# Retention, then a two-layer network, on one core: the last sums reordered and stored in halves, and the last tokens' input copied by two engines

## The chip, the cores and the metric

The kernel runs on one core of a Trainium2 chip. A core has TensorE (matrix products into PSUM), VectorE, ScalarE, GpSimd and SyncE, each with an instruction queue of its own that is worked off in order; engines wait for one another by semaphores. DMAs are issued here from the queues of SyncE and ScalarE (and GpSimd, early on). The metric is the time of one execution on the device, in microseconds (us).

## The reference

```python
def _attn_ref(q, k, v):                       # 8 x 8 x 576 x 64, float32
    scores = (1.0 / np.sqrt(D_)) * np.matmul(q, k.transpose(0, 1, 3, 2))
    gamma = 1.0 - 2.0 ** (-5.0 - np.arange(H))
    Dmat = np.where(rel >= 0, gamma[:, None, None] ** rel[None, :, :], 0.0)   # rel = pos_i - pos_j
    return np.matmul(scores * Dmat[None], v)

def _moe_ref(x, w_in, w_out, alpha):          # x: 4608 x 512, the heads side by side
    h = x @ w_in                              # 4608 x 2048
    s = np.sin(alpha * h)
    g = h + s * s / (alpha + 1e-09)
    return g @ w_out                          # 4608 x 512
```

So each token goes through a causal retention (decay per head), and then through two matrix products with a snake activation between them.

## The kernel before

**Blocks.** The 4608 tokens are worked in nine blocks of 512. Blocks 0 to 7 are the first 512 tokens of each of the eight sequences; block 8, the "ends", gathers the last 64 tokens of all eight. For each block the retention makes the transposed input of the network: `xT` (for block 8 `xS`, four slabs of 128 x 512 in float16). The network's first product runs in 16 units of 128 hidden features (`project`, L554, matmuls on L562): four matmuls of 128x512 sum up one PSUM bank `hps`. ScalarE takes the sine of it (`sine`, L570), ScalarE or VectorE squares that (`square`, L579/L581), and VectorE makes `gT = ss * inva + hps` (`product`, L586), in float16.

**The second product** of blocks 3 to 8 is made from seven products of quarter size instead of eight (`part_product`, L659, matmuls on L671; `FACTORS` names the two factors of each). `row_sum` (L644, VectorE on L652) makes the sums of `gT` that four of the seven take as left factor, and `after_product` (L700) puts the results together: product 1 becomes `low` (ScalarE, L703), product 6 gives `mid = acc + low` (L705), product 7 gives a new `low` (L707), and products 2, 3, 4 and 5 each complete one quarter of the block's output in a tile `osb` (L720), which `store` (L677) sends to the output in two DMAs, one for each half of the partitions (issued on L684 for block 8, on L688 for the others). With `more=True`, used once, product 5 is also added to `mid` (L716), for product 3's quarter needs it: `osb(3) = acc(3) + mid`.

**Order.** The whole kernel lies in a manual schedule: each engine's instructions stand in the order in which the program names them. A loop over blocks n = 3 to 8 names, for each pair of units, the first product of block n and one quarter-size product of block n - 1. `unit_start` (L1351) issues a unit's matmuls and sine and whatever `at_unit` has put there; `unit_end` (L1357) issues the square, the `product`, and then what `behind` has put there. In block 7 the retention of the ends is made (class `Ends`, L469): `Ends(0)` covers four sequences, `Ends(2)` the other four, each with a PSUM tile of its own. At unit 13 their matmuls are issued (L510 and L528), and L1348 puts the four copies from PSUM into `xS` (`keep`, L535, through `copy`, L118; L120 on ScalarE, L122 on VectorE) behind units 13 and 14: the two of `Ends(0)` behind unit 13, the two of `Ends(2)` behind unit 14, all on ScalarE. Block 8's first `project` reads all of `xS`. In block 7, unit 14 ends only after unit 15 has started and the quarter-size product 4 of block 6 has been handled (L1398 to L1404).

**The end** (L1406 to L1427) makes the seven products of block 8 with no first product left beside them, in the order 2, 4, 1, 6, 7, 5, 3. Stores there are issued from two queues, `both` = SyncE's for partitions 0 to 63 and ScalarE's for 64 to 127. Product 3 is made in two column halves (js = 0, 1) in two PSUM banks; VectorE sums each half into `osb(3)` as it is finished, and one `store` behind both sends the 128 x 512 tile: two DMAs of 64 partitions x 2 x 256 float32, 128 KB each.

Of the kernel before, what the change touches and what calls it, by code (L numbers as in the profile page):

```python
# [12 lines left out]
ADD = mybir.AluOpType.add  # L13
# [23 lines left out]
def kernel(  # L37
# [18 lines left out]
    nc = tc.nc  # L56
# [49 lines left out]
    V, A_, G_ = nc.vector, nc.scalar, nc.gpsimd  # L106
# [8 lines left out]
    def halves(n):  # L115
        return slice(64 * n, 64 * n + 64)
# [542 lines left out]
    def part_product(n, i, tag, js=(0, 1), first=None):  # L659
        left, right = FACTORS[i]  # L660
        if tag is not None:
            parts[n, i] = bank(tag)
        else:
            parts[n, i] = parts[n, first]
        acc = parts[n, i]
        for j in js:
            for p in range(2):
                lhs = piece(left, p) if isinstance(left, str) else quarter(n, *left, p)
                rhs = piece(right, p) if isinstance(right, str) else w_quarter(*right, p)
                for x in range(4):  # L670
                    matmul(  # L671
                        acc[:, 256 * j : 256 * j + 256], lhs[:, x, 128 * j : 128 * j + 128], rhs[:, x],
                        start=(tag is not None and j == js[0] and p == 0 and x == 0),
                        stop=(p == 1 and x == 3), skip_group_check=True,
                    )

    def store(n, t, e, osb, js=(0, 1), issue=(nc.sync, nc.sync)):  # L677
        cols = slice(256 * e, 256 * e + 256)
        for r in range(2):
            if n == 8:  # L680
                b0 = 4 * t + 2 * js[0]
                dst = out.rearrange("(b s) d -> b s d", s=S)[b0 : b0 + 2 * len(js), 512:576, cols]
                dst = dst.rearrange("(j r) s d -> r s j d", r=2)
                issue[r].dma_start(dst[r], osb[halves(r), js[0] : js[-1] + 1])  # L684
            else:
                r0 = 576 * n + 256 * t + 128 * js[0]
                dst = out[r0 : r0 + 128 * len(js), cols].rearrange("(j i r) d -> r i j d", r=2, i=64)
                issue[r].dma_start(dst[r], osb[halves(r), js[0] : js[-1] + 1])  # L688

    kept = {}  # L690
# [4 lines left out]
    def kept_tile(name):  # L695
        tag = {"low": "qT1", "mid": "u2"}[name]
        kept[name] = work.tile([P, 512], F32, tag=tag, bufs=1, name=name)
        return kept[name]

    def after_product(n, i, js=(0, 1), issue=(nc.sync, nc.sync), apart=False, more=False):  # L700
        acc = parts[n, i]
        if i == 1:
            nc.scalar.copy(kept_tile("low"), acc)  # L703
        elif i == 6:
            nc.vector.tensor_tensor(kept_tile("mid"), acc, kept["low"], ADD)  # L705
        elif i == 7:
            nc.vector.tensor_tensor(kept["low"], acc, kept["mid" if apart else "low"], ADD)  # L707
        else:
            t, e = {2: (0, 0), 3: (0, 1), 4: (1, 0), 5: (1, 1)}[i]
            cols = slice(256 * js[0], 256 * js[-1] + 256)  # L710
            if (n, i) not in kept:
                kept[n, i] = work.tile([P, 2, 256], F32, tag="osb", bufs=4, name="osb")
            osb = kept[n, i].rearrange("p j d -> p (j d)")
            source = kept["mid" if i == 3 else "low"]
            if more:
                nc.vector.tensor_tensor(kept["mid"], acc, kept["mid"], ADD)  # L716
            if i == 2 and not apart:
                nc.scalar.copy(osb[:, cols], acc[:, cols])
            else:
                nc.vector.tensor_tensor(osb[:, cols], acc[:, cols], source[:, cols], ADD)  # L720
            if issue:
                store(n, t, e, kept[n, i], js, issue)

    at = [Attention(b) for b in range(B)]
    zero = work.tile([P, 512], F16, tag="zero", bufs=1, name="zero")
# [57 lines left out]
    with tc.manual_schedule():  # L783
# [485 lines left out]
        for n in range(3, NBLK):  # L1269
# [4 lines left out]
            def at_unit(u, *fs):  # L1274
                todo.setdefault(u, []).extend(fs)

            def behind(u, *fs):
                after.setdefault(u, []).extend(fs)
# [59 lines left out]
            if n == 7:  # L1338
                for i in range(PAD):
                    at_unit(3 + i, fill_up)  # L1340
                E = (Ends(0), Ends(2))
                at_unit(7, lambda: E[0].scores(next(m)), lambda: E[1].scores(next(m)))
                at_unit(7, E[0].masked)
                behind(7, E[1].masked)
                at_unit(13, lambda: E[0].values(False, next(m)), lambda: E[1].values(False, next(m)))
                at_unit(13, lambda: E[0].values(True), lambda: E[1].values(True))
                at_unit(13, E[0].add_states, E[1].add_states)
                for i in range(4):  # L1348
                    behind(13 + i // 2, lambda i=i: E[i // 2].keep(i % 2, A_))

            def unit_start(i, u, tag):  # L1351
                project(n, u, tag)
# [38 lines left out]
            for i in range(8):  # L1391
                for u in (2 * i, 2 * i + 1):
                    unit_start(u, units[u], aside.get(u) or next(h))
                    if u % 2 and slots[i] is not None:
                        k_ = slots[i]
                        part_product(n - 1, k_, None if k_ in (2, 7, 3) else "op", first={2: 1, 7: 6, 3: 5}.get(k_))
                        after_product(n - 1, k_)
                    if n < 8 and u == 14:  # L1398
                        square(n, u, A_)
                        continue  # L1400
                    if n < 8 and u == 15:
                        product(n, 14)
                        for f in after.get(14, []):
                            f()  # L1404
                    unit_end(u, units[u], None if A and u == 13 else V if u in ON_V else A_)
        n = NBLK - 1  # L1406
        both = (nc.sync, nc.scalar)
# [3 lines left out]
        row_sum(n, "S2", 1, V)  # L1411
        part_product(n, 1, "op")
        after_product(n, 1)
        part_product(n, 6, next(h))
        row_sum(n, "S1", 1, V)
        after_product(n, 2, apart=True, issue=both)
        row_sum(n, "S4", 1, V)
        after_product(n, 6)
# [4 lines left out]
        after_product(n, 5, more=True, issue=both)  # L1423
        for j, tag in enumerate(("m0", "op")):
            part_product(n, 3, tag, (j,))
            after_product(n, 3, (j,), None)
        store(n, 0, 1, kept[n, 3], issue=both)  # L1427


# [28 lines left out]
```

## Time and profile before

| what | value |
|---|---|
| time, three runs | 296.99, 298.12 (the median), 298.87 us |
| the profiled execution | 297.58 us, of which the span from first to last instruction is 295.9 us |
| mean granted TensorE clock | 0.996 |
| busy: PE / VectorE / ScalarE / GpSimd | 283.5 / 225.0 / 204.9 / 135.9 us |
| busy from 252 to 291 us (39 us: block 8) | PE 38.43, VectorE 32.70, ScalarE 18.82 us |
| from 291 us to the end (4.9 us) | PE 0, VectorE 0.28 us |

How the lines of a profile are read: times are us from the start of the span, durations in us or ns where marked. In a timeline, a row gives start, duration, engine, line, operation, output tile <- input tiles, shapes, and how many instructions are merged in the row (x8); brackets at its end give the idle time of the engine just before the row and who ended it. PE is TensorE's matmul row, PEld its weight loads (which run ahead of the matmuls), DVE is VectorE, ACT ScalarE, POOL GpSimd, SPq and ACTq the DMA-issuing queues of SyncE and ScalarE. A group line of the page gives busy time and mean duration after the bar. Matmuls overlap one another and their ends are modelled, so the distance between two starts says more than a duration.

### The profile page before, as it was taken

How to read it: one execution, taken by the hardware profiler on the slowest of the kernel's cores; microseconds unless marked ns; L12 is line 12 of the kernel's file. 1: busy time of each engine (PE TensorE's matmuls, PEld its weight loads, DVE VectorE, ACT ScalarE, POOL GpSimd, SP SyncE). 2: the span in 40 equal slices, each digit the busy share in tenths (PEclk: the TensorE clock that was granted, in tenths of full speed). 3: DMA queues.
4: the chain of work that ended last, by engine and by line, in shares of the span. 5: the costliest groups of instructions: out<-in, count | busy, mean ns of one | idle time of the engine just before them, and what ended most of it. 6: DMA issues, size and time to landing. Idle time of an engine off the chain costs nothing.

```text
span 295.9 us, 8497 instructions
## 1 busy us (share of the span) xinstructions
PE 283.5 (96%) x3480; PEld 183.5 (62%) x3480; DVE 225.0 (76%) x334; ACT 204.9 (69%) x343; POOL 135.9 (46%) x151
## 2 busy tenths in 40 slices
PE   6789999999999999999999999999999999999993
PEld 4566545555544644455777767767767776676782
DVE  2596978788348889697977697769777986977883
ACT  2579935997594887786767976887688657865500
POOL 5693678565688685560497049704950000000000
PEclk9999999999999999999999999999999999999998
DMA  7999999998798778999979777988753103111213
GB/s 216 347 234 210 248 296 321 243 259 241 177 226 176 175 164 174 253 161 194 146 178 218 147 168 189 218 146 198 179 133 79 40 13 78 35 38 35 71 38 107
DMA packets 123400, 50.09 MB, mean 169 GB/s; under 512 B 80353, under 2 KB 121313, under 8 KB 123361
## 3 DMA queue, kind: packets, MB, share of 16 engines
q1 hardware_dynamic: 119424, 44.78, 65.1%
q0 software_dynamic: 2688, 4.19, 7.8%
q10 hardware_dynamic: 1248, 0.58, 0.7%
q8 instruction: 27, 0.44, 0.6%
q14 instruction: 13, 0.10, 0.1%
HBM read 36.75 MB, written 9.44 MB: 156 GB/s over the span
## 4 chain that ended last, share of the span: by engine, by line
PE 80%; DMA 10%; POOL 3%; ACT 3%; SPq 1%; issue 1%; DVE 0%; POOLq 0%; ACTq 0%
PE hps L562 39%; PE hps L671 24%; PE ops L605 9%; DMA raw<-in_v_dram 3%; DMA w_in<-in_moe_w_in_dram 3%; PE o L427 2%; DMA raw<-in_k_dram 2%; PE sc L385 2%; DMA qT<-q 2%; PE kv L321 1%; POOL q L207 1%; ACT s L570 1%; POOL k L207 1%; PE o L449 1%; SPq L158 1%
## 5 line engine op out<-in xcount | busy, mean ns | idle before, releaser
L586 DVE SCALAR_TENSOR_TENSOR gT<-ss,inva,hps 128x512 f16<-128x512 f16 x144 | 105.7, 744 | 31.1 <-ACT ss L579 27.5
L570 ACT ACTIVATE s<-hps,alpha_t 128x512 f16<-128x512 f32 x144 | 96.8, 680 | 46.0 <-PE hps L562 45.7
L562 PE MATMUL hps<-xT,w_in 128*128 128x512 f16 (+1 forms) x532 | 121.0, 372 | 0.5 <-DMA w_in<-in_moe_w_in_dram 0.5
L562 PEld LDWEIGHTS <-w_in 128*128 128x128 f16 x596 | 66.6, 114 | 50.3 <-DMA w_in<-in_moe_w_in_dram 0.6
L579 ACT ACTIVATE ss<-s 128x512 f16<-128x512 f16 x107 | 67.3, 630 | 2.8
L605 PE MATMUL ops<-w_out,gT 128*128 128x512 f16 x192 | 46.8, 380 | 0.0
L671 PEld LDWEIGHTS <-gT 128*128 128x128 f16 x384 | 37.5, 98 | 8.3
L207 POOL TENSOR_TENSOR k<-raw,cn 128x1024 f16<-128x1024 f32 (+1 forms) x17 | 29.6, 1746 | 8.5 <-DMA raw<-in_k_dram 8.5
L671 PEld LDWEIGHTS <-S 128*128 128x128 f16 x288 | 27.7, 98 | 5.3
L605 PEld LDWEIGHTS <-gT 128*128 128x128 f16 x192 | 17.9, 98 | 20.4
L359 POOL TENSOR_TENSOR s<-kvs,cn 128x256 f16<-128x256 f32 x17 | 10.4, 612 | 38.9 <-DVE S L652 36.0
L207 POOL TENSOR_TENSOR q<-raw,cn 128x1024 f16<-128x1024 f32 x13 | 24.9, 1919 | 7.3 <-DMA raw<-in_q_dram 4.3
L671 PE MATMUL hps<-T,gT 128*128 128x256 f16 x192 | 22.9, 273 | 0.0
L671 PE MATMUL hps<-w_out,gT 128*128 128x256 f16 x192 | 22.9, 273 | 0.0
L671 PE MATMUL hps<-w_out,S 128*128 128x256 f16 x192 | 22.8, 273 | 0.0
L397 DVE TENSOR_TENSOR ret<-sc,mask 128x1024 f16<-128x1024 f32 x16 | 19.2, 1220 | 1.9 <-PE sc L385 1.9
L367 POOL TENSOR_TENSOR kvs<-s,kvs 128x256 f32<-128x256 f32 x21 | 16.7, 797 | 3.6 <-DVE kvs L122 1.1
L720 DVE TENSOR_TENSOR osb<-hps,low 128x512 f32<-128x512 f32 x13 | 9.0, 691 | 10.6 <-PE hps L671 10.6
L581 DVE TENSOR_TENSOR ss<-s 128x512 f16<-128x512 f16 x29 | 13.4, 465 | 3.4 <-ACT s L570 3.4
L366 POOL TENSOR_TENSOR s<-kvs,cn 128x256 f32<-128x256 f32 x21 | 12.8, 612 | 6.6 <-ACT kvs L120 6.4
L652 DVE TENSOR_TENSOR S<-gT,S 128x1024 f16<-128x1024 f16 x24 | 15.5, 684 | 0.0
L562 PE MATMUL hps<-xS,w_in 128*128 128x512 f16 x64 | 15.1, 379 | 0.4 <-ACT xS L120 0.4
(82 smaller groups left out, 270.7 us busy)
## 6 DMA issues: line engine op xcount, KB each, us to landing
out_dram<-osb SPq DMA_DIRECT2D x68, 128.0 KB, 2.6
raw<-in_q_dram SPq DMA_DIRECT2D x16, 512.0 KB, 6.3
raw<-in_k_dram SPq DMA_DIRECT2D x8, 512.0 KB, 5.9
raw<-in_v_dram SPq DMA_DIRECT2D x8, 512.0 KB, 6.4
raw<-in_v_dram SPq DMA_DIRECT2D x32, 128.0 KB, 3.1
raw<-in_k_dram SPq DMA_DIRECT2D x32, 128.0 KB, 3.1
w_in<-in_moe_w_in_dram POOLq DMA_DIRECT2D x4, 512.0 KB, 11.6
w_out<-in_moe_w_out_dram POOLq DMA_DIRECT2D x4, 512.0 KB, 12.9
```

What stands on the lines that cost most here:

```text
L207: eng.tensor_tensor(dst[:, a0:a1].rearrange("p a r t d -> p t (a r) d"), t_.rearrange("p (t a) x -> p t a x", t=2)[:, :, a0:a1].rearrange( ...
L366: nc.gpsimd.tensor_tensor(s32, self.kvs[:, c - 1], g1.unsqueeze(2).to_broadcast([P, 4, D]), MULT)
L367: nc.gpsimd.tensor_tensor(self.kvs[:, c], s32, self.kvs[:, c], ADD)
L397: nc.vector.tensor_tensor(ret.rearrange("p t (z x) -> p (t z) x", z=2)[:, :, 0:n], sc.rearrange("p t (z x) -> p (t z) x", z=2)[:, :, 0:n], ...
L562: matmul(hps_of[n, fc][0][:, cols], w_in16[fc // 4][:, a, fc % 4 :: 4], xs[n][:, a, cols], start=(a == 0 and part != 1), stop=(a == KT - 1 ...
L570: nc.scalar.activation(s_t, hps, mybir.ActivationFunctionType.Sin, bias=0.0, scale=alpha_t[:, fc : fc + 1],)
L579: nc.scalar.activation(ss_t, s_t, mybir.ActivationFunctionType.Square)
L581: eng.tensor_tensor(ss_t, s_t, s_t, MULT)
L586: nc.vector.scalar_tensor_tensor(gT[n][:, fc, :], ss_t, inva[:, fc : fc + 1], hps, MULT, ADD)
L605: matmul(ops[n, c, cols.start][:, cols], gT[n][:, fk, c * P : (c + 1) * P], w_out16[:, fk, cols], start=(fk == 0), stop=(fk == FC - 1), sk ...
L652: return eng.tensor_tensor(out_, x, y, op)
L671: matmul(acc[:, 256 * j : 256 * j + 256], lhs[:, x, 128 * j : 128 * j + 128], rhs[:, x], start=(tag is not None and j == js[0] and p == 0 ...
```

## The change

Three things are edited.

1. In `after_product`, VectorE's addition to `mid` (only with `more`, product 5 of block 8) comes behind product 5's own sum and its store, not ahead of them.
2. Product 3 of block 8 stores each column half as soon as its sum is made: two times two DMAs of 64 partitions x 256 float32 (64 KB each), in place of two DMAs of 128 KB behind both halves.
3. The two `xS` copies of `Ends(2)` go from ScalarE to VectorE, and from behind unit 14 of block 7 to behind unit 13, where those of `Ends(0)` stand and stay. On VectorE they come behind the first half-sum `S3` of block 7 (L652) and ahead of the sum of product 4 of block 6 (L720). TensorE's wait for them moves to the weight load of block 8's first matmul, and names VectorE now.

```diff
@@ after_product
-            if more:
-                nc.vector.tensor_tensor(kept["mid"], acc, kept["mid"], ADD)
             if i == 2 and not apart:
                 nc.scalar.copy(osb[:, cols], acc[:, cols])
             else:
                 nc.vector.tensor_tensor(osb[:, cols], acc[:, cols], source[:, cols], ADD)
-            if issue:
-                store(n, t, e, kept[n, i], js, issue)
+            store(n, t, e, kept[n, i], js, issue)
+            if more:
+                nc.vector.tensor_tensor(kept["mid"], acc, kept["mid"], ADD)
@@ block 7
                 for i in range(4):
-                    behind(13 + i // 2, lambda i=i: E[i // 2].keep(i % 2, A_))
+                    behind(13, lambda i=i: E[i // 2].keep(i % 2, V if i // 2 else A_))
@@ the end
         for j, tag in enumerate(("m0", "op")):
             part_product(n, 3, tag, (j,))
-            after_product(n, 3, (j,), None)
-        store(n, 0, 1, kept[n, 3], issue=both)
+            after_product(n, 3, (j,), both)
```

On TensorE and GpSimd the order of the instructions stays as it was.

## The prediction

> **What bounds the kernel now.** I read the chain of work that ended last first, then the timeline of the two places the change touches, then waits and DMA landings. The chain from 258 us on:
>
> ```profile
> 278.59 12.24 PE hps L671 x112
> 290.83 0.02 issue
> 290.86 0.42 DVE osb L720
> ```
>
> TensorE's products run without a break up to 290.83, then one VectorE sum, then the stores. So two things can shorten this stretch: a hole in TensorE's work, and what lies behind its last matmul. All of TensorE's waits for data from 200 us on are one line:
>
> ```profile
> PE hps L562 <- ACT xS L120: 0.4, 1, 0.4
> ```
>
> That is block 8's first matmul, waiting for ScalarE's last `xS` copies. The timeline there:
>
> ```profile
> 248.50 1.05 ACT L120 CAST xS<-os 128x512 f16<-128x512 f32 x2
> ...
> 249.29 0.68 DVE L652 TENSOR_TENSOR gT<-gT 128x1024 f16<-128x1024 f16 x1
> ...
> 250.08 1.91 PE L671 MATMUL hps<-T,gT 128*128 128x256 f16 x16
> ...
> 250.71 0.67 ACT L570 ACTIVATE s<-hps,alpha_t 128x512 f16<-128x512 f32 x1
> 251.28 1.06 ACT L120 CAST xS<-os 128x512 f16<-128x512 f32 x2
> 251.72 0.11 PEld L562 LDWEIGHTS <-w_in 128*128 128x128 f16 x1
> 252.03 0.69 DVE L720 TENSOR_TENSOR osb<-hps,low 128x512 f32<-128x512 f32 x1 [2.05 <-PE hps L671]
> ...
> 252.39 1.89 PE L562 MATMUL hps<-xS,w_in 128*128 128x512 f16 x8 [0.40 <-ACT xS L120]
> ...
> 254.11 1.91 PE L671 MATMUL hps<-w_out,gT 128*128 128x256 f16 x16
> ...
> 255.86 1.89 PE L562 MATMUL hps<-xS,w_in 128*128 128x512 f16 x8
> ```
>
> A group of 16 L671 matmuls hands over to the next unit in 255.86 - 254.11 = 1.75 us. The group at 250.08 should have done so at 251.83; the matmul began at 252.39. The hole is 0.56 us (0.40 of it marked idle). ScalarE's copies end at 252.34, just before. VectorE meanwhile is idle for 2.05 us before its L720, waiting for TensorE.
>
> **Edit 3, the copies.** VectorE takes two copies behind its L652, which ends at 249.29 + 0.68 = 249.97. The `Ends` matmuls are done then, for ScalarE's first copies began at 248.50. The nearest rows for such a copy on VectorE, same shape and types, and twice the width:
>
> ```profile
> L122 DVE CAST xT<-o 128x512 f16<-128x512 f32 x5 | 3.3, 685 | 0.1
> L122 DVE CAST xT<-o 128x1024 f16<-128x1024 f32 x1 | 1.2, 1225 | 1.3 <-PE o L449 1.3
> ```
>
> Two by 685 ns is 1.37 us: they end at 251.34, 0.49 before TensorE could use them (251.83) and 0.69 before VectorE's L720 can start (its matmuls end at 250.08 + 1.91 = 251.99). So they lie wholly in VectorE's 2.05 us of idle time and cost nothing; that cover would be gone if each took over 0.93 us (for TensorE) or 1.0 us (for L720). On ScalarE 1.06 us of copies leave, and the square behind them runs up to 0.94 us earlier; its product on VectorE stays behind L720, which doesn't move, so nothing is gained by that. The hole closes: **-0.56 us**; bounds 0 and -0.56.
>
> Does it last to the end? TensorE would run 0.56 us ahead of VectorE, which from 252.03 is in arrears:
>
> ```profile
> 252.63 0.74 DVE L586 SCALAR_TENSOR_TENSOR gT<-ss,inva,hps 128x512 f16<-128x512 f16 x1
> ...
> 257.87 0.69 DVE L652 TENSOR_TENSOR S<-gT 128x1024 f16<-128x1024 f16 x1
> ...
> 261.06 1.15 PE L671 MATMUL hps<-T,S 128*128 128x256 f16 x9
> ...
> 261.78 0.75 DVE L586 SCALAR_TENSOR_TENSOR gT<-ss,inva,hps 128x512 f16<-128x512 f16 x1 [0.24 <-ACT ss L579]
> ...
> 263.01 0.69 DVE L705 TENSOR_TENSOR mid<-hps,low 128x512 f32<-128x512 f32 x1 [0.48 <-PE hps L671]
> ```
>
> The matmuls at 254.11 reuse the bank that L720 reads until 252.72; moved to 253.55 they still have 0.83 us to spare. Those at 261.06 need the sum that L652 has at 258.56: 2.5 us, 1.9 after the shift. From 261.78 on VectorE idles for others again (0.24, then 0.48), so it has caught up by then. I keep all 0.56.
>
> **Edits 1 and 2, the end.** The timeline of VectorE and the issues, and the durations of single issues:
>
> ```profile
> 287.16 3.66 PE L671 MATMUL hps<-w_out,S 128*128 128x256 f16 x32
> 287.36 0.69 DVE L707 TENSOR_TENSOR low<-hps,mid 128x512 f32<-128x512 f32 x1 [0.98 <-PE hps L671]
> 288.09 0.69 DVE L720 TENSOR_TENSOR osb<-hps,low 128x512 f32<-128x512 f32 x1
> ...
> 289.11 0.69 DVE L716 TENSOR_TENSOR mid<-hps,mid 128x512 f32<-128x512 f32 x1 [0.33 <-PE hps L671]
> 289.72 0.68 DVE L720 TENSOR_TENSOR osb<-hps,low 128x512 f32<-128x512 f32 x1
> 290.31 0.97 DVE L720 TENSOR_TENSOR osb<-hps,mid 128x256 f32<-128x256 f32 x2
> ```
>
> ```profile
> 290.43 0.60 SPq L684 DMA_DIRECT2D out_dram<-osb  x1
> 290.43 0.63 ACTq L684 DMA_DIRECT2D out_dram<-osb  x1
> 291.31 0.60 SPq L684 DMA_DIRECT2D out_dram<-osb  x1
> 291.31 0.66 ACTq L684 DMA_DIRECT2D out_dram<-osb  x1
> L598 SPq DMA_DIRECT2D out_dram<-osb x24: 517/593/1676, 68.2 to 145.2; - x24
> ```
>
> I reckon on the clock of this trace, before the shift of 0.56. Product 5's sum takes the place of L716 at 289.11 and its two stores go out at 289.82, 0.61 us sooner. `mid` follows at 289.72. The first half of product 3 must now wait for the instruction just ahead of it; such a pair (L707, then L720) starts 288.09 - 287.36 = 0.73 apart, so it runs from 290.45 (0.14 later) to 290.87. The second half could start at 290.86 by TensorE, and starts at 290.87: its end stays, at 291.29 against 291.28. Edit 1 alone moves nothing at the end; it clears the queues for edit 2.
>
> The first half's stores are issued at 290.90. Each queue issues one at a time, so the second half's, ready at 291.31, wait until 290.90 + 0.60 = 291.50 on SyncE's and 290.90 + 0.66 = 291.56 on ScalarE's queue. A store of 64 rows like these (L598) takes 0.52 to 0.59 to issue, so halving the bytes saves little there. **The last issue moves from 291.31 to 291.56: +0.25.** No row shows a 64 KB store landing. The rows around it, from issue to landing:
>
> ```profile
> gate<-w_out SPq DMA_DIRECT2D x10, 16.0 KB, 2.0
> out_dram<-osb SPq DMA_DIRECT2D x6, 128.0 KB, 2.4
> out_dram<-osb SPq DMA_DIRECT2D x1, 128.0 KB, 2.5
> DMA to landing us min/median/max: 2.9/2.9/2.9
> ```
>
> The third is the store issued at 288.80 with its twin beside it and nothing ahead; the fourth is the last one, at 291.31, whose data lay behind those issued at 290.43. So the last landing before is 294.21, and 1.65 us of closing work follow to 295.86. Half the bytes lie between 16 KB (2.0) and 128 KB (2.5), and nothing is ahead of them by then: product 5's stores have left 0.61 us sooner, and the first half's 128 KB, issued 0.66 before, is half of what a pair of 128 KB moves. I take the middle, 2.25: landing at 293.81, so **-0.40 us**. Bounds: a quick issue and 2.0 (291.42 + 2.0 = 293.42, so -0.8), and the old 2.9 kept (294.46, so +0.25).
>
> [...]
>
> **Sum.** -0.56 - 0.40 = -0.96 us on the profiled execution's 297.58: 296.62. That execution lies 0.54 below the median of the runs (298.12), from which the same sum gives 297.16. I predict the middle, **296.9 us**.
>
> **Rivals.**
>
> (a) *The tail gives nothing.* The second store waits behind the first in both queues, and its landing costs 2.9 as before because the constant part rules: +0.25, in all -0.31, so 297.3 to 297.8 by the two starting points, 297.5 in the middle. For it: 16 KB already costs 2.0. Against: the 2.9 stood behind another pair.
>
> (b) *The hole stays.* Block 8's first matmul waits for something else at that time, VectorE late by its arrears; then only the tail's -0.40 remains: 297.2 to 297.7. Against: VectorE's row shows 2.05 us of idle time where the copies go.
>
> (c) *Slower.* The copies on VectorE cost what the row twice as wide costs, 1.225 each: they end at 249.97 + 2.45 = 252.42. TensorE starts no sooner than before (+0.03), and L720 with all of VectorE's arrears is put off by 0.39, which the bank reuse at 254.11 (slack 1.39 unshifted) takes without harm; with the tail's +0.25 this is +0.28, so 297.9 to 298.4. It decides above about 1.2 us for a copy. Against: five rows of just this shape at 685 ns.
>
> (d) *The change does nothing that shows*: the three runs of before lie 1.88 us apart, more than the whole sum. This is no other mechanism, but it sets the range.
>
> **How the numbers follow.** Forecast 0.67, (a) 0.18, (b) 0.08, (c) 0.04, and 0.03 for what I have not seen. The range takes the sum's bounds (-1.36 to +0.28) from either starting point, 296.2 to 298.4, and something for the scatter of single runs below: 295.7 to 298.3. One per cent is 3.0 us, about what a measurement of this kernel can tell from no change; no case reaches it, the sum of the best bounds being -1.36 and (c) +0.28. So within 1%: 0.95; faster 0.02 and slower 0.03 are left for what I have not seen and for the scatter.
>
> **What would show it.** In the new profile: two L122 copies `xS` on DVE of about 0.69 each from 249.9 on; no wait of PE on `xS`, and block 8's first matmul near 251.8; the last L671 group ending near 290.3; product 5's sum ahead of the `mid` sum, its stores 0.6 sooner relative to TensorE's end; four L684 issues of 64 KB, the last beginning about 0.7 after TensorE's end instead of 0.48; the span near 294.9. Wrong would be: copies longer than 0.93 us, a PE wait on DVE anywhere after 252, issues of half stores much shorter than 0.5 us (a larger gain), or a last landing 2.6 or more after its issue (no gain in the tail).

## The result, and the profile after

| | before | changed |
|---|---|---|
| median of 20 runs, us | 298.47 (296.99 to 300.76) | 296.66 (295.29 to 299.69) |
| ratio to before, 95% interval | | 0.9943 [0.9917, 0.997] |
| profiled execution / its span, us | 297.58 / 295.9 | 296.62 / 294.9 |

The changed kernel is faster by 0.57% (0.3 to 0.8%), 1.7 us of 298.47 (0.9 to 2.5). The forecast of 296.9, within 1% of before, holds.

First the hole ahead of block 8, in the timeline of the changed kernel:

```profile
250.12 0.68 DVE L652 TENSOR_TENSOR gT<-gT 128x1024 f16<-128x1024 f16 x1
250.72 1.28 DVE L122 CAST xS<-os 128x512 f16<-128x512 f32 x2
250.72 1.91 PE L671 MATMUL hps<-T,gT 128*128 128x256 f16 x16
...
252.47 1.89 PE L562 MATMUL hps<-xS,w_in 128*128 128x512 f16 x8
252.67 0.69 DVE L718 TENSOR_TENSOR osb<-hps,low 128x512 f32<-128x512 f32 x1 [0.67 <-PE hps L671]
```

The two copies stand on VectorE in its idle time, 1.28 us together; 0.67 of the 2.05 us of idle time is left ahead of the next sum. Block 8's first matmul starts 252.47 - 250.72 = 1.75 us behind the product ahead of it, where it was 2.31, and carries no wait. The profile names no wait of TensorE for data from 200 us to the end.

Then the end, again the timeline of the changed kernel; the issues are cut to single rows:

```profile
287.24 3.66 PE L671 MATMUL hps<-w_out,S 128*128 128x256 f16 x32
...
289.19 0.69 DVE L718 TENSOR_TENSOR osb<-hps,low 128x512 f32<-128x512 f32 x1 [0.33 <-PE hps L671]
289.80 0.68 DVE L721 TENSOR_TENSOR mid<-hps,mid 128x512 f32<-128x512 f32 x1
290.57 0.79 DVE L718 TENSOR_TENSOR osb<-hps,mid 128x256 f32<-128x256 f32 x2
```

```profile
289.91 0.60 SPq L684 DMA_DIRECT2D out_dram<-osb  x1
289.91 0.64 ACTq L684 DMA_DIRECT2D out_dram<-osb  x1
291.02 0.49 SPq L684 DMA_DIRECT2D out_dram<-osb  x1
291.03 0.51 ACTq L684 DMA_DIRECT2D out_dram<-osb  x1
291.60 0.56 SPq L684 DMA_DIRECT2D out_dram<-osb  x1
291.63 0.80 ACTq L684 DMA_DIRECT2D out_dram<-osb  x1
```

TensorE ends at 290.90 (287.24 + 3.66), against 290.82 before. Measured from there, product 5's stores go out at -0.99 in place of -0.39, and the last stores at 0.70 and 0.73 in place of 0.49. The span ends 4.0 us after TensorE in place of 5.04.

So the two spans differ by -0.56 (hole) - 1.04 (end) = -1.60 us, and by +0.64 the other way for what lies ahead of 250 us and was not changed (the product at 250.08 stands at 250.72 here); together -0.96, the difference of the profiled spans. The -1.60 agrees with the -1.7 (0.9 to 2.5) of the timed runs.

### The profile page after: what moved, and what is told of

It is laid out like the page before. It is cut to its first block, busy times and chain, and to the rows that moved or that the text cites. A ratio compares the mean times of both kernels' runs of the same rounds, so it can differ in the third digit from the quotient of the medians.

```text
span 294.9 us, 8502 instructions
## 1 busy us (share of the span) xinstructions
PE 283.0 (96%) x3480; PEld 183.2 (62%) x3480; DVE 225.4 (76%) x336; ACT 204.1 (69%) x341; POOL 135.8 (46%) x151
## 5 line engine op out<-in xcount | busy, mean ns | idle before, releaser
L652 DVE TENSOR_TENSOR S<-gT,S 128x1024 f16<-128x1024 f16 x24 | 15.5, 684 | 0.0
L397 DVE TENSOR_TENSOR ret<-sc,mask_halved 128x768 f16<-128x768 f32 x16 | 15.2, 950 | 0.0
```

Source lines behind the costliest of these rows:

```text
L397: nc.vector.tensor_tensor(ret.rearrange("p t (z x) -> p (t z) x", z=2)[:, :, 0:n], sc.rearrange("p t (z x) -> p (t z) x", z=2)[:, :, 0:n], ...
L652: return eng.tensor_tensor(out_, x, y, op)
```

## The experiments

All runs are set out in one table, from the records of their profiles, in us. "Hole" is the distance from the start of the last quarter-size product ahead of block 8 to block 8's first matmul; "block 8" is from there to TensorE's end. The other columns count from TensorE's end: the start of the last issue, the last landing of a store, from that landing to the end of the span ("closing"), and the whole tail. A DMA counts as landed with the last step of its semaphore.

| kernel | hole | block 8 | last issue | last landing | closing | tail |
|---|---|---|---|---|---|---|
| before | 2.31 | 38.43 | 0.50 | 3.57 | 1.48 | 5.04 |
| changed | 1.75 | 38.43 | 0.73 | 3.01 | 0.99 | 4.00 |
| changed, second profile | 1.75 | 38.43 | 0.73 | 3.03 | 0.98 | 4.01 |
| edit 3 alone | 1.75 | 38.43 | 0.49 | 3.54 | 1.48 | 5.02 |
| edits 1 and 2 alone | 2.50 | 38.43 | 0.73 | 3.00 | 0.98 | 3.98 |
| all copies on ScalarE, early | 1.75 | 38.43 | 0.49 | 3.55 | 1.48 | 5.03 |
| two copies on VectorE, late | 5.24 | 40.11 | 0.49 | 3.58 | 1.48 | 5.05 |
| edit 1 alone | 2.50 | 38.43 | 0.49 | 3.24 | 1.48 | 4.72 |
| edit 2 alone | 2.50 | 38.43 | 1.24 | 3.48 | 0.99 | 4.47 |
| before, two loads more | 2.34 | 38.43 | 0.50 | 3.99 | 0.99 | 4.98 |
| changed, two loads more | 1.75 | 38.43 | 0.73 | 3.29 | 1.39 | 4.68 |
| before, more waits on SyncE | 2.50 | 38.43 | 0.49 | 3.55 | 1.48 | 5.03 |
| changed, three queues | 1.75 | 38.43 | 0.70 | 3.02 | 0.99 | 4.01 |

At the end, the parts of like kernels repeat within 0.04; the hole is 1.75 in every kernel with all copies at the early place, and 2.31 to 2.50 where ScalarE makes two of them at the old place. Whole times of one kernel lie up to 5 us apart, and five of the kernels (edit 1 alone, edit 2 alone, both with two loads more, more waits on SyncE) have a single execution; so the parts carry the verdicts.

**The changed kernel again** (no edit).

> The changed kernel itself, for a second profile. My account of the two profiles: the distance from the start of the last quarter-size product ahead of block 8 to block 8's first matmul falls from 2.31 to 1.75 us (hole closed, -0.56); from TensorE's last matmul to the last store's landing 3.55 falls to 3.01 (-0.54); from the last landing to the end of the span 1.48 falls to 0.97 (-0.51, not foreseen). Theory A (closing work depends on where in SyncE's row of closing waits the last store's semaphore stands): about 0.97 again. Rival B (the 0.51 is a chance delay of one profile): anything from 0.9 to 1.5. Time: about -1.6 us against before by the three parts, 0.995.

Measured: ratio 0.9951 [0.9916, 0.9986]; closing 0.98 again. The short closing is no chance of one profile.

**Edit 3 alone.**

```diff
-                    behind(13 + i // 2, lambda i=i: E[i // 2].keep(i % 2, A_))
+                    behind(13, lambda i=i: E[i // 2].keep(i % 2, V if i // 2 else A_))
```

> Edit 3 alone on the kernel before. Theory: the hole closes in full, 2.31 falls to 1.75 us, and nothing at the end changes (5.0 to 5.1 us from TensorE's last matmul to the end of the span): -0.56 us, ratio 0.998. Rival: VectorE's arrears pass the gain on as a later wait, so that TensorE has a new wait behind block 8's first units and the stretch from there to the end is longer by as much: 0.

Measured: 0.9985 [0.9942, 1.0027]; hole 1.75, tail as before, and "block 8" the same 38.43. The gain is not handed on as a wait. The timing alone could not have told it from zero.

**Edits 1 and 2 alone.** On the changed kernel, the copies go back:

```diff
-                    behind(13, lambda i=i: E[i // 2].keep(i % 2, V if i // 2 else A_))
+                    behind(13 + i // 2, lambda i=i: E[i // 2].keep(i % 2, A_))
```

> Edits 1 and 2 alone. Theory: the hole stays at 2.31 us; from TensorE's last matmul to the end of the span about 4.0 us in place of 5.0 to 5.1: -1.0 us, ratio 0.9965. By the prediction's own sum it is -0.40: 4.6 to 4.7 us.

Measured: 0.9993 [0.9951, 1.0036], which takes in both the expected 0.9965 and nothing; tail 3.98, so -1.06 at the end, and not the -0.40 of the prediction. The hole is 2.50 here: with the old place of the copies it lies between 2.31 and 2.50 in six profiles, so edit 3 is worth 0.56 to 0.75.

**The place or the engine?** Two kernels change one and not the other. First the place alone, all four copies on ScalarE behind unit 13:

```diff
-                    behind(13 + i // 2, lambda i=i: E[i // 2].keep(i % 2, A_))
+                    behind(13, lambda i=i: E[i // 2].keep(i % 2, A_))
```

> The kernel before, with all four copies behind unit 13 but all on ScalarE: place changed, engine not. Theory (the place counts): ScalarE copies from 248.5 to about 250.6 on the clock of before, the sine of unit 14 is 1.1 us later and still in time for its product, block 8's first matmul waits for nothing: 2.31 falls to 1.75 us, -0.56, as with two engines. Rival (the second engine counts): ScalarE's sines and squares of units 14 and 15 come late by 1.1 us, VectorE's products with them, and TensorE waits later: no gain, or up to +0.5.

The timeline of this kernel:

```profile
250.58 2.03 ACT L120 CAST xS<-os 128x512 f16<-128x512 f32 x4
...
252.10 1.91 PE L671 MATMUL hps<-T,gT 128*128 128x256 f16 x16
252.48 0.72 ACT L570 ACTIVATE s<-hps,alpha_t 128x512 f16<-128x512 f32 x1
...
253.85 1.89 PE L562 MATMUL hps<-xS,w_in 128*128 128x512 f16 x8
```

Measured: 0.9965 [0.9928, 1.0002]; hole 1.75. ScalarE's next sine runs after the copies, and still nothing waits for it. Then the engine alone, at the old place:

```diff
-                    behind(13 + i // 2, lambda i=i: E[i // 2].keep(i % 2, A_))
+                    behind(13 + i // 2, lambda i=i: E[i // 2].keep(i % 2, V if i // 2 else A_))
```

> The kernel before with the two copies on VectorE but at their old place, behind unit 14 of block 7: engine changed, place not. Theory (the place counts): on VectorE that place is behind the sum of product 4 of block 6, the product of unit 14 and a half-sum, so the copies run from 253.9 to 255.3 on the clock of before; block 8's first matmul comes about 3.5 us after it could, in place of 0.56: the distance from the product ahead of it rises from 2.31 to about 5.2 us, and the kernel is about 2.9 us slower (1.010), TensorE's way from there to its end unchanged at 38.43. Rival (the second engine counts): a gain as with both.

Its TensorE waits, its timeline, and three stretches of it. In the last view a row gives the stretch and its length, the busy time of PE, PEld, DVE, ACT and POOL with their instructions in brackets, and then TensorE's clock, the DMA share and GB/s:

```profile
PE hps L562 <- DVE xS L122: 3.3, 1, 3.3
```

```profile
255.07 0.68 DVE L652 TENSOR_TENSOR S<-gT 128x1024 f16<-128x1024 f16 x1
255.68 1.28 DVE L122 CAST xS<-os 128x512 f16<-128x512 f32 x2
256.88 0.74 DVE L586 SCALAR_TENSOR_TENSOR gT<-ss,inva,hps 128x512 f16<-128x512 f16 x1
...
257.10 2.80 PE L562 MATMUL hps<-xS,w_in 128*128 128x512 f16 x8 [3.33 <-DVE xS L122]
```

```profile
257.00:258.00 1.00, 0.90 (x5) 0.49 (x6) 1.00 (x2) 0.00 (x0) 0.00 (x0) 0.97 0.07 18
258.00:261.30 3.30, 3.30 (x13) 1.77 (x12) 2.16 (x4) 2.00 (x3) 0.00 (x0) 0.50 0.00 0
261.30:263.00 1.70, 1.70 (x14) 1.27 (x13) 0.00 (x0) 0.54 (x2) 0.00 (x0) 0.99 0.00 0
```

Measured: 1.0224 [1.0169, 1.028], not the 1.010 expected. The hole is 5.24, as worked out. What was not foreseen: TensorE, idle for 3.33 us, then has half its clock until 261.3 us, and block 8 takes 40.11 in place of 38.43 (+1.68). The two make +4.6 us, 1.015. In the profiled execution 1.78 us more lie ahead of the edited place (the last product there starts at 251.86, and at 250.08 before); what the timed runs show beyond the 1.015 stays open. The place decides; the second engine isn't needed, and at the wrong place it harms.

**Edit 1 alone**, on the kernel before:

```diff
-            if more:
-                nc.vector.tensor_tensor(kept["mid"], acc, kept["mid"], ADD)
...
             if issue:
                 store(n, t, e, kept[n, i], js, issue)
+            if more:
+                nc.vector.tensor_tensor(kept["mid"], acc, kept["mid"], ADD)
```

> Edit 1 alone: product 5's sum ahead of the addition to mid, one store of product 3 as before. Theory: product 5's stores go out 0.6 us sooner, the last issue is where it was, its data has nothing ahead of it, so the last landing comes 2.5 instead of 2.9 to 3.1 us after its issue: from TensorE's last matmul to the end 4.6 to 4.7 us in place of 5.0 to 5.1. By the prediction's words (edit 1 alone moves nothing at the end): 5.0 to 5.1.

Measured: tail 4.72, -0.32, all of it in the landing (3.24). In the DMA records, product 5's data is through at 1.56 us after TensorE's end (2.01 in the kernel before), and the data of the last stores, issued at the same 0.49, runs from 1.74 to 2.89 in place of 1.96 to 3.10. So about 0.2 is data that product 5's no longer holds up. The other 0.1 lies between the last packet and the landing (0.36 in place of 0.47); its cause is not shown.

**Edit 2 alone**, on the kernel before:

```diff
-            after_product(n, 3, (j,), None)
-        store(n, 0, 1, kept[n, 3], issue=both)
+            after_product(n, 3, (j,), both)
```

> Edit 2 alone: two half stores of product 3, with the addition to mid still ahead of product 5's sum. Theory: product 5's stores hold the queues until 291.05, the first half's until 291.55 and the second half's are issued only then, 0.3 us later than the one store before, with less data: from TensorE's last matmul to the end 4.6 to 5.0 us, so edit 2 needs edit 1 to give its whole gain. Rival (the smaller store alone brings it): about 4.0 us as with both.

Measured: tail 4.47, below the 4.6 to 5.0 expected, but well above the rival's 4.0. The half stores queue behind product 5's, and the last is issued 1.24 after TensorE's end, 0.74 later than the single store; the landing still comes 0.09 sooner, and the closing is 0.49 shorter. Edits 1 and 2 bring -0.32 and -0.57 apart and -1.04 together.

**Where does the closing come from?** Behind the last store, SyncE has twelve semaphore records in the profile of before (on L1453) and twelve in that of the changed kernel (on L1451). The waits on the semaphores of its DMAs and ScalarE's stand in the same order in both (100, 102, 103, 106 to 110), and most steps from one wait to the next behind data that has landed take 0.06 to 0.08 us. Two 16 KB loads into an unused tile, ahead of block 8's last products, move the last stores by two places in that order and change nothing of the work:

```diff
         part_product(n, 2, "m0")
         part_product(n, 4, next(h))
+        for _ in range(2):
+            fill_up()
```

In the kernel before:

> The kernel before, with two 16 KB loads into the unused gate tile put on SyncE's queue ahead of block 8's last products: nothing but the semaphores of the last stores changes, by two places, so that the last ones stand last in SyncE's row of closing waits, as in the changed kernel. Theory A (the place in the row counts): from the last landing to the end about 1.0 us in place of 1.48. Rival B (chance): 1.0 to 1.5, whatever the place. Rival C (it hangs on the store itself or on TensorE's clock, whose record falls to a half at 293.3 in the kernel before and not in the changed one): 1.48.

and in the changed one:

> The changed kernel with the same two loads: its last stores then have the first semaphores in the row of closing waits, with six waits behind them at 0.065 us each. Theory A: from the last landing to the end about 1.3 to 1.4 us in place of 0.97. Rival B (chance) and C (the store or the clock): 0.97, or no order in it.

Measured: closing 0.99 for the first and 1.39 for the second, as theory A has it, and against the store as the cause, for the first has the large stores and the short closing. The clock is ruled out by two other kernels: with edits 1 and 2 alone, all of the closing of 0.98 has half the clock, and with all copies early on ScalarE, a closing of 1.48 has the full clock up to its last 0.2 us. In the second kernel here, the waits behind the last landing follow at 0.06 to 0.09 us each. But both kernels' last landing is later too (3.99 against 3.57, and 3.29 against 3.01), so the first gains almost nothing. Their data isn't late: its last packet ends at 3.11 (3.10 in the kernel before) and at 2.64 (2.66 in the changed one). What is late is the last of the sixteen steps of the semaphore, 0.24 and 0.22 behind the fifteenth, where all other kernels show 0.05 at most. In these two alone, an 8 KB packet of the queue that the profile calls "instruction" runs while the steps come in (3.06 to 3.37, and 2.57 to 3.35). Whether it delays the step was not tried.

The order alone doesn't give 0.49. In the kernel before, the step from the wait on ScalarE's last store to the next takes 0.40 us, where 0.06 to 0.08 is usual. Such a step of 0.39 to 0.41 stands in every other profile but one, always into SyncE's record number 335 (counted from 0), whichever wait that is (in the one, the changed kernel with two loads more, that record waits for the last landing): the one on the last SyncE store in the kernel before (343 SyncE records), two waits earlier in the changed one (345), three earlier with two loads more (346). One further kernel was to move it alone, by waits on work long done, ahead of the last stores:

```diff
-        part_product(n, 4, next(h))
+        told(part_product(n, 4, next(h)), nc.sync)        # it returns its last matmul
...
-        row_sum(n, "S2", 1, V)
+        told(row_sum(n, "S2", 1, V), nc.sync)
...
-            nc.scalar.copy(kept_tile("low"), acc)
+            done = nc.scalar.copy(kept_tile("low"), acc)
+            if n == 8:
+                told(done, nc.sync)
```

> The kernel before with a few more waits in SyncE's stream ahead of the last stores, on work of TensorE, ScalarE and VectorE that is long done: nothing else changes, the stores keep their semaphores. Theory S (a pause of 0.33 us stands at a fixed count of SyncE's instructions; in the kernel before it falls behind the last landing, with two instructions more it falls ahead of it): from the last landing to the end 1.48 falls to about 1.15, the three waits behind it remain. Rival P (only the place of the last store's semaphore counts, and the pause belongs to the wait that follows it): 1.48.

Measured: 1.48. But SyncE's records stayed 343, so that the added waits made none of their own, and the long step stayed at 335. So the run says nothing against S, and the place was not tried apart. By position, an estimate from these steps, the 0.49 splits into about 0.33 for the long step (0.40 in place of 0.07), which in the changed kernel falls 0.65 ahead of the last landing (at 2.36 us, the landing at 3.01), and 0.16 for two waits fewer behind it.

**Three queues**, for what is left at the end:

```diff
-            after_product(n, 3, (j,), both)
+            after_product(n, 3, (j,), ((nc.sync, nc.gpsimd), (nc.scalar, nc.sync))[j])
```

> The changed kernel with the four half stores on three queues: the first half on SyncE's and GpSimd's, the second on ScalarE's and SyncE's, so that only one of the second half's stores has to stand behind another. If what still costs at the end is the second half's wait in the queues (0.24 us of 0.73), ScalarE's store goes out 0.49 in place of 0.73 us after TensorE's last matmul and lands at about 2.8; SyncE's stays at 0.70 and lands at 2.85: from TensorE's end to the end 3.85 in place of 4.0. If GpSimd's path is slow (its loads took 11.6 to 12.9 us for 512 KB, no row shows 64 KB), its store lands last and the tail is 4.0 or more.

Measured: 0.994 [0.9908, 0.9973]; tail 4.01, as in the changed kernel. GpSimd's store landed at 2.65 and ScalarE's at 2.82, both in good time. SyncE's, issued at 0.70 as in the changed kernel, landed at 3.02 and not at the 2.85 that it has there, so the 3.85 expected for the tail was missed. Its data starts as before (1.98, and 1.96 in the changed kernel) but is through 0.19 later (2.56, and 2.37), with ScalarE's data beside it until 2.38. So a sooner issue alone doesn't bring a sooner end here; whether the data beside it is the cause was not tried apart.

## Why the prediction was right, point by point

- *The whole number.* The forecast holds, and luck has a part in it. The profiled execution came to 296.62, to the hundredth what the sum gives from the first starting point, but only because two misses of 0.64 us offset each other: the end gave that much more than reckoned, and the part ahead of 250 us, which no edit touched, took that much more. So block 8 began at 252.47 and TensorE ended at 290.90, not near the 251.8 and 290.3 that were to show it, while the span is the 294.9 that was named. The forecast also started low: from the 298.47 of twenty runs, -0.96 leads to 297.5, and the measured -1.7 (0.9 to 2.5) only just takes in -0.96. (The upper end of the stated range, 298.3, lies 0.1 below what its own sum gives; nothing hangs on it.)
- *The hole closes: -0.56.* Right in mechanism and size: 2.31 to 1.75, and it lasts to the end, with "block 8" at 38.43 on both sides. The copies took 1.28 together where 1.37 was reckoned.
- *Two engines.* The prediction followed the cover on VectorE and didn't ask whether ScalarE could have made the copies at the early place. It could.
- *Edit 1 alone moves nothing at the end.* Wrong: -0.32. It leaves the last issue where it was, as the prediction said, but the last store's data comes sooner, with product 5's out of its way. The text used just this when it came to edit 2.
- *The last issue moves by +0.25.* Right: 0.49 to 0.73. In its parts, small misses offset each other: the first half's stores went out at 0.12 where 0.07 was reckoned, took 0.49 and 0.51 to issue in place of 0.60 and 0.66, and the next began 0.09 behind their ends.
- *A half store lands 2.25 after its issue.* Right for the last two: 2.15 on SyncE's queue, 2.28 on ScalarE's. The first half's, behind product 5's, took 2.41 and 2.56. The landing is 3.01 after TensorE's end, where 2.98 follows from the sum.
- *-0.40 for the tail.* This is the term that was mis-sized: it measured -1.04. Two readings failed. The 2.9 us taken for the old landing was SyncE's store; ScalarE's, issued beside it, landed at 294.38, 0.17 later, so the landing gained 0.56. And the "1.65 us of closing work" was taken as a constant, without a look at what it consists of; it fell by 0.49.
- Rivals: (a) fell, for the landing did come sooner; (b) and (c) fell, with no wait on `xS` and copies of 0.64 each. The scatter that (d) names is real; only 20 runs for each side, and the parts of the profiles, told the gain from nothing.

## What to carry to other kernels

A copy that TensorE waits for is first moved ahead in its own engine's order, to where its input is ready; a second engine is the next question. At the end of a kernel, count from TensorE's last matmul through every store of every queue to its landing, look at whose data lies ahead in the queues, and treat the closing (0.98 to 1.48 us here) as work that has an order of its own. Gains of 0.3 us are read from such distances, which repeat to 0.04, and not from whole times that scatter by 5.

## What the runs showed of the hardware

**Where TensorE had half its clock.** Besides the case above (idle for 3.33 us, then 0.50 from 258.0 to 261.3), four profiles have it early on, in a part that no edit touched: TensorE waits for a transposed tile at about 90 us. In the kernel before it waits 0.8 us, in the changed one 1.4, and the clock is 1.00 there and behind (to 97 us in the one, to 94.2 in the other). In edit 2 alone the wait was 2.6 us, in the changed kernel with two loads more 2.7, in "more waits on SyncE" 2.8 and in "three queues" 2.2, and the clock record of each of the four then shows 0.50 for 3.41 us. The wait in the kernel before and in "more waits on SyncE", and of the latter the 3.41 us with the wait (clock 1.00) and the 3.41 us behind them (0.50):

```profile
PE sc L385 <- DMA qT<-q: 0.8, 1, 0.8
```

```profile
PE sc L385 <- DMA qT<-q: 2.8, 1, 2.8
```

```profile
88.62:92.03 3.41, 0.64 (x33) 0.51 (x32) 2.52 (x4) 0.46 (x2) 2.17 (x2) 1.00 1.15 257
```

```profile
92.03:95.44 3.41, 3.41 (x20) 1.19 (x9) 2.47 (x3) 0.00 (x0) 3.25 (x4) 0.50 0.68 150
```

But in edit 1 alone the same wait was 2.4 us, longer than the 2.2 of "three queues", and the clock was 1.00 in the two stretches around it:

```profile
86.45:89.86 3.41, 2.20 (x11) 0.78 (x8) 2.92 (x5) 2.48 (x7) 2.29 (x2) 1.00 0.92 199
89.86:93.27 3.41, 2.21 (x40) 1.37 (x41) 1.75 (x2) 0.00 (x0) 2.28 (x2) 1.00 0.93 201
```

So the length of the wait alone does not tell these five apart; what does was not tried apart.

The four came to the product ahead of block 8 at 252.4 to 254.7 us; the profiles without a halved clock between 20 us and there came at 250.1 to 252.3. By estimate, 3.41 us at half the clock are up to 1.7 us of this scatter of 4.6, so part of it and not all.

**One step of SyncE near its end took about 0.33 us longer than its neighbours.** In twelve of the thirteen profiles, the step into SyncE's record 335 takes 0.39 to 0.41 us where 0.06 to 0.08 is usual, with 343 to 346 records in all: 0.40 in the kernel before (343 records), 0.39 in the changed one (345). In nine of the twelve, an 8 KB packet of the "instruction" queue starts 0.63 to 0.66 us after that record (0.64 in the kernel before, 0.65 in the changed one; 0.76, 0.90 and 1.32 in the other three). Whether the two belong together, and what the long step is, was not settled.
